# Layer normalisation of five row tiles moved to GpSimd, statistics in one stretch, scheduler numbers refitted

## Chip, cores and metric

One core of one Trainium2 chip. The metric is the device time of one execution in microseconds, the slowest core (here the only one). The kernel before took 181.99 us (median of 3 runs, 181.78 to 183.0).

## The reference, cut to what matters

```python
def _layernorm(x, axis=-1, eps=1e-5):
    m = jnp.mean(x, axis=axis, keepdims=True)
    v = jnp.var(x, axis=axis, keepdims=True)
    return (x - m) / jnp.sqrt(v + eps)

# A: gated long convolution over S = 2048 for each of D = 640 channels (by Fourier transform)
# B: token-mixing MLP
h = _layernorm(x)                                        # x: (1, 2048, 640)
u = gelu(einsum("bsd,sf->bdf", h, w1) + b1)              # w1: (2048, 1536)
y = einsum("bdf,fs->bds", u, w2) + b2
# result: g * a + (1 - g) * y^T,  g = sigmoid(sum(x * gate_w))
```

`x` lies in SBUF as 16 row tiles of 128 x 640 in bf16, called X, four to each block `hk`. The first MLP product adds over the 2048 rows, so a finished sum needs all 16 normalised tiles.

## The kernel before

The whole kernel is one list of operations. Before anything is emitted, a list scheduler *in the kernel file* walks it with assumed durations and writes the order in which each engine will execute. At run time each engine keeps that order and waits on semaphores. So a wrong duration does not change what is computed; it changes the order.

The parts that matter:

```python
free = {e: 2.4 if e == "ACT" else 0.0 for e in engs}     # when each engine begins, in the model
dma_free = 0.0
...
def ts(eng, o, a, s1, s2, op0, op1=None, mode=1, prio=None, extra=0.0):
    n = n_of(o)
    d = dve_dur(n, mode) + extra if eng == "DVE" else n / 900.0 + 0.2    # assumed us on GpSimd
    ...
def ln_tile(hk, p):      # two bn_stats of 320 columns and one bn_aggr, VectorE
    ...
def ln_scale(a, b):      # GpSimd: var + eps, power -0.5, and their product
    ...
def ln_apply(a, b):      # VectorE: X = (X - mean) * rstd, one tile each
    ...
# for h in (0, 1): transp(h, db) ...; after the first half's transposes
#   consts()             # PE turns the bias rows b1, b2, which come by small DMAs
#   fwd(...)             # forward Fourier products of the filter ("W")
for t in range(8):
    ln_tile(t // 4, t % 4)
for t in range(8, 12):
    ln_tile(t // 4, t % 4)
lnlast.append(SC.ops[-1])
ln_scale(0, LNA)                       # LNA = 8
ln_apply(0, LNA)
lnlast.append(SC.ops[-1])
for t in range(12, 16):
    for o_ in ln_tile(t // 4, t % 4):
        o_.after.update(lnlast[-1:])
ln_scale(LNA, 16)
ln_apply(LNA, 16)
lnlast.append(SC.ops[-1])
```

## Time and profile before

| | before |
|---|---|
| time, median | 181.99 us |
| span in the profile | 179.7 us |
| PE busy / idle | 173.1 / 6.6 us |
| first unbroken forward product (chain of waits) | 13.18 us |
| PE's last matmul ends | 177.06 us |
| X tiles 0 to 3 normalised | about 21.4 us |
| X tiles 8 to 15 normalised | 30.1 to 33.0 us |

PE and DVE (VectorE) are both near 95% busy. ACT is ScalarE, POOL is GpSimd. "GT" is the gelu's output, "ksh" the shifted keys, "wT" the turned filter, "rows" the bias rows, "rstd" the inverse deviation.

### The profile page before, as it was taken

The page shows a single profiled execution, that of the slowest core. Times are in us where ns is not written, and L with a number is a line of the kernel's source. Part 1 is how long each engine was busy: PE and PEld are TensorE (multiplying, and loading weights), DVE is VectorE, ACT ScalarE, POOL GpSimd, SP SyncE. Part 2 cuts the span into 40 slices and gives each one's busy share as a digit, 9 for nine tenths or more (in the row PEclk, how much of TensorE's full clock was granted, in tenths as well). Part 3 has the DMA queues.
Part 4 walks back from the last instruction along what each step waited for, and adds up shares of the span by engine and source line. Part 5 has one row for each costly group of instructions (what it writes and reads, how often), then busy time and mean ns, then how long its engine had stood idle before and what let it go on. Part 6 is the DMA issues. An engine that isn't in the chain of part 4 may idle for free.

```text
span 179.7 us, 3335 instructions
## 1 busy us (share of the span) xinstructions
PE 173.1 (96%) x1381; PEld 128.7 (72%) x1381; DVE 171.2 (95%) x203; ACT 116.9 (65%) x176; POOL 43.7 (24%) x42
## 2 busy tenths in 40 slices
PE   7969998899999999999999999999999999999993
PEld 2546785587778777776777778888888887777772
DVE  7999895999999999999999899999999999999984
ACT  5899998899898999617999932131231323753760
POOL 4089404190000054000240010402525000252000
PEclk9999999999999999999999999999999999999999
DMA  6999999999999999998299969797999999599463
GB/s 151 381 411 372 388 294 194 268 420 296 212 258 286 184 271 248 229 228 218 60 243 299 197 94 365 170 225 253 166 193 217 210 200 385 218 154 240 116 233 135
DMA packets 38542, 43.51 MB, mean 242 GB/s; under 512 B 15867, under 2 KB 31360, under 8 KB 38528
## 3 DMA queue, kind: packets, MB, share of 16 engines
q1 hardware_dynamic: 33296, 32.16, 58.2%
q0 software_dynamic: 5200, 11.14, 35.6%
q8 instruction: 11, 0.18, 0.4%
q14 instruction: 3, 0.02, 0.0%
q10 hardware_dynamic: 32, 0.01, 0.0%
HBM read 25.87 MB, written 2.62 MB: 159 GB/s over the span
## 4 chain that ended last, share of the span: by engine, by line
PE 88%; ACT 10%; DVE 0%; issue 0%
PE pp L295 88%; ACT wT L670 3%; ACT C L670 2%; ACT ksh L670 2%; ACT FTB L670 2%; ACT L670 1%; ACT GT L670 0%; DVE O L682 0%; DVE zz L686 0%; ACT cw L670 0%; DVE cst L686 0%
## 5 line engine op out<-in xcount | busy, mean ns | idle before, releaser
L295 PE MATMUL pp<-X,ring 128*128 128x320 bf16 x384 | 55.6, 299 | 0.0
L626 DVE TENSOR_TENSOR C<-C 128x2560 bf16<-128x2560 bf16 (+2 forms) x37 | 54.5, 1521 | 0.0
L295 PE MATMUL pp<-GT,W 128*128 128x320 bf16 x384 | 52.6, 299 | 0.0
L295 PEld LDWEIGHTS pp<-GT,W 128*128 128x128 bf16 x384 | 43.6, 114 | 8.6
L295 PEld LDWEIGHTS pp<-X,ring 128*128 128x128 bf16 x384 | 37.1, 98 | 14.9 <-DVE X L641 0.7
L670 ACT ACTIVATE C<-pp 128x640 bf16<-128x640 f32 x64 | 40.4, 723 | 4.9 <-PE pp L295 4.9
L670 ACT ACTIVATE O<-pp,c,omg 128x640 bf16<-128x640 f32 x15 | 13.3, 884 | 34.7 <-PE pp L295 34.7
L264 POOL DMA_DIRECT2D C<-C x8 | 10.9, 1610 | 41.7 <-DVE C L626 38.3
L295 PE MATMUL pp<-wT,FTB 128*128 128x320 bf16 x112 | 17.2, 299 | 2.5 <-ACT wT L670 1.4
L670 ACT ACTIVATE cgb<-pp,gg 128x640 bf16<-128x640 f32 x16 | 12.7, 794 | 5.7 <-PE pp L295 5.3
L295 PEld LDWEIGHTS pp<-wT,FTB 128*128 128x128 bf16 x112 | 10.5, 98 | 7.7 <-ACT wT L670 1.8
L670 ACT ACTIVATE GT<-pp,cc 128x640 bf16<-128x640 f32 x12 | 9.6, 799 | 9.0 <-PE pp L295 9.0
L626 DVE TENSOR_TENSOR tm<-C,C 128x2560 bf16<-128x2560 bf16 (+1 forms) x7 | 14.3, 2057 | 0.0
L922 DVE BATCH_NORM_STATS2 stats<-X 128x6 f32<-128x320 bf16 x32 | 13.5, 461 | 0.0
L295 PE MATMUL pp<-C,FTB 128*128 128x320 bf16 x96 | 13.4, 299 | 0.0
L264 POOL DMA_DIRECT2D C<-q_hi x6 | 5.9, 977 | 27.7 <-DVE C L626 13.2
L295 PEld LDWEIGHTS pp<-C,FTB 128*128 128x128 bf16 x96 | 9.3, 98 | 3.8 <-issue 0.3
L670 ACT ACTIVATE gq<-gq 128x640 bf16<-128x640 bf16 x16 | 11.8, 741 | 0.0
L626 DVE TENSOR_TENSOR SS<-C 128x2560 bf16<-128x2560 bf16 x8 | 11.7, 1487 | 0.1
L626 DVE TENSOR_TENSOR C<-tm 128x2560 bf16<-128x2560 bf16 (+1 forms) x9 | 10.6, 1192 | 0.1
L670 ACT ACTIVATE ksh<-pp 128x1024 bf16<-128x1024 f32 (+1 forms) x12 | 9.8, 894 | 0.6 <-PE pp L295 0.6
L670 ACT ACTIVATE wT<-pp 128x1024 bf16<-128x1024 f32 x10 | 9.7, 1041 | 0.6 <-PE pp L295 0.6
(73 smaller groups left out, 193.4 us busy)
## 6 DMA issues: line engine op xcount, KB each, us to landing
ring<-in_B_w_dram SPq DMA_DIRECT2D x12, 512.0 KB, 9.6
W<-in_B_w_dram SPq DMA_DIRECT2D x12, 512.0 KB, 6.5
C<-C POOLq DMA_DIRECT2D x8, 640.0 KB, 10.6
X<-in_A_q_dram SPq DMA_DIRECT2D x4, 640.0 KB, 8.4
kn<-in_A_k_dram SPq DMA_DIRECT2D x4, 640.0 KB, 9.3
out_dram<-O SPq DMA_DIRECT2D x7, 320.0 KB, 3.5
C<-SS POOLq DMA_DIRECT2D x3, 640.0 KB, 11.4
ssm<-in_A_ssm_k_dram SPq DMA_DIRECT2D x3, 512.0 KB, 6.8
```

The lines of the kernel that those rows point to most:

```text
L264: ins = engobj.dma_start(out_ap, in_ap, accum_op=ALU.add, max_dma_last_dim=2560)
L295: ins = self.nc.tensor.matmul(ps_ap, lhsT=lhsT, rhs=rhs, start=start, stop=stop, skip_group_check=True)
L626: o_ = SC.add(eng, d, lambda s: T.op(eng, lambda e: e.tensor_tensor(o, a, b, op), rd, [o]), rd, [o], prio=prio, name="tt")
L670: return T.op("ACT", lambda e: e.activation(o, src, func, **kw), rr + [src], ww)
L922: ops.append(SC.add("DVE", 0.38, (lambda o, i: lambda s: T.op("DVE", lambda e: e.bn_stats(o, i), [i], [o]))(o, i), [i], [o]))
```

## The change

Its intent: GpSimd is free from 20 to 28 us. Let it normalise tiles 0 to 4 while VectorE finishes all statistics, so VectorE does not stop between two stretches and has five tiles fewer to normalise. The scheduler's numbers are fitted to the trace at the same time: the engines' beginnings, load rates, the lengths of the transposes, iota and memset costs.

```diff
-        free = {e: 2.4 if e == "ACT" else 0.0 for e in engs}
+        free = {"ACT": 2.93, "DVE": 0.85, "POOL": 0.83, "PE": 1.18, "SP": 0.0, "QA": 0.0}
-        dma_free = 0.0
+        dma_free = 0.3
 ... (ssm_load, x_load: assumed rates)
-  rate=(262.0 if a == 0 else 195.0) if h == 0 else 385.0)
+  rate=({0: 262.0, 1: 223.0}.get(a, RL3)) if h == 0 else 385.0)      # RL3 = 394.0
-  rate=410.0)
+  rate=(352.0 if hk == 0 else 415.0))
 ... (transp: assumed length)
-            m_.dur = 0.5
+            m_.dur = (0.65 + 0.31 * SPIN[db] if h == 0 else 0.55)
 ... (iota, memset: no port lock in the model, iota by its size)
-                for t in range(8):
+                for t in range(16):
                     ln_tile(t // 4, t % 4)
-                for t in range(8, 12):
-                    ln_tile(t // 4, t % 4)
-                lnlast.append(SC.ops[-1])
-                ln_scale(0, LNA)
-                ln_apply(0, LNA)
-                lnlast.append(SC.ops[-1])
-                for t in range(12, 16):
-                    for o_ in ln_tile(t // 4, t % 4):
-                        o_.after.update(lnlast[-1:])
+                    if t == LNA - 1:
+                        ln_scale(0, LNA)
+                lnst = SC.ops[-1]
                 ln_scale(LNA, 16)
-                ln_apply(LNA, 16)
+                for t in PAP:                      # PAP = (0, 1, 2, 3, 4)
+                    xs = X[:, t // 4, t % 4, :]
+                    ts("POOL", xs, xs, mv[:, t, 0:1], rstd[:, t:t + 1], ALU.subtract, ALU.mult, prio=0)
+                lnlast.append(lnst)
+                for t in range(16):
+                    if t not in PAP:
+                        ln_apply(t, t + 1)
                 lnlast.append(SC.ops[-1])
```

More of the change, by code (lines that the diff above doesn't have):

```diff
@@ L683, in last_stt, with nolock @@
             return SC.add("DVE", dve_dur(n_of(o), 1), emit, [sc, b], [o], vt=vt, name="fin")
+        def nolock(*a, **k):
+            o_ = SC.add(*a, **k)
+            o_.lock = False
+            return o_
         def memset(eng, ap, val, prio=None):
-            return SC.add(eng, 0.2, lambda s: T.op(eng, lambda e: e.memset(ap, val), [], [ap]), [], [ap], prio=prio)
+            return nolock(eng, 0.2, lambda s: T.op(eng, lambda e: e.memset(ap, val), [], [ap]), [], [ap], prio=prio)
         def mms(vt, items, prio=None, name="mm"):
@@ L729, in ssm_load @@
         def ssm_load(h, a, b):
-            dma(ssm[:, a:b, 1024 * h:1024 * h + 1024], dr(A_ssm_k, 128 * S * a + 1024 * h, [[S, 128], [128 * S, b - a], [1, 1024]]), 128 * (b - a) * 2048, chain=True, rate=(262.0 if a == 0 else 195.0) if h == 0 else 385.0)
+            dma(ssm[:, a:b, 1024 * h:1024 * h + 1024], dr(A_ssm_k, 128 * S * a + 1024 * h, [[S, 128], [128 * S, b - a], [1, 1024]]), 128 * (b - a) * 2048, chain=True, rate=({0: 262.0, 1: 223.0}.get(a, RL3)) if h == 0 else 385.0)
+        RL3 = 394.0
         def row8(t, hk):
@@ L738, in x_load @@
         def x_load(hk):
-            dma(X[:, hk, :, :], dr(A_q, 512 * hk * D, [[4 * D, 128], [1, 4 * D]]), 128 * 5120, chain=True, rate=410.0)
+            dma(X[:, hk, :, :], dr(A_q, 512 * hk * D, [[4 * D, 128], [1, 4 * D]]), 128 * 5120, chain=True, rate=(352.0 if hk == 0 else 415.0))
         def w1_load(c, hk):
@@ L792, in _build @@
         memset("DVE", cst[:, 1:2], -0.5)
-        iota = lambda ap, pat, b, cm: SC.add("POOL", 0.2, lambda s: T.op("POOL", lambda e: e.iota(ap, pat, base=b, channel_multiplier=cm), [], [ap]), [], [ap])
+        iota = lambda ap, pat, b, cm: nolock("POOL", 0.1 + n_of(ap) / 1100.0, lambda s: T.op("POOL", lambda e: e.iota(ap, pat, base=b, channel_multiplier=cm), [], [ap]), [], [ap])
         iota(dif[:, :], [[1, 128]], 0, -1)
@@ L942, in _build @@
         LNA = 8
+        PAP = tuple(range(5))
         lnlast = []
```

## The prediction

> **What bounds the kernel now.** I read the page first: TensorE (PE) is busy for 96% of the span and VectorE (DVE) for 95%, so neither figure alone says which of them sets the end. The chain of the work that ended last, in order of time, decides:
>
> ```profile
> 13.18 16.41 PE pp L295 x142
> ...
> 30.36 2.02 PE pp L295 x12
> ...
> 32.41 1.30 ACT C L670 x2
> ...
> 33.72 1.28 ACT L670
> ...
> 35.02 0.79 ACT GT L670
> 35.81 1.78 ACT C L670 x3
> 37.59 3.29 ACT ksh L670 x4
> ...
> 40.93 136.12 PE pp L295 x1048
> ...
> 177.08 0.55 DVE O L682
> ```
>
> Columns are start, length and what ran. From 40.93 us to 177.05 the chain is one piece of matmuls, ended by half a microsecond of VectorE. To see whether that piece has slack I cut the span into stages and asked for busy time by stage:
>
> ```profile
> 0.00:13.18 13.18, 10.53 (x74) 5.28 (x74) 12.19 (x34) 10.40 (x11) 5.53 (x12) 1.00 0.86 312
> 13.18:20.80 7.62, 7.62 (x59) 5.39 (x60) 7.02 (x25) 7.01 (x13) 6.85 (x6) 1.00 1.07 378
> 20.80:29.00 8.20, 8.20 (x83) 6.63 (x82) 7.14 (x20) 7.48 (x10) 0.85 (x2) 1.00 1.06 300
> 29.00:41.00 12.00, 10.68 (x124) 7.48 (x122) 10.92 (x15) 10.51 (x15) 6.21 (x3) 1.00 0.99 311
> 41.00:177.06 136.06, 136.04 (x1048) 103.93 (x1048) 133.37 (x111) 81.55 (x129) 24.29 (x21) 1.00 0.94 221
> ```
>
> The columns are the window, its length, then busy time and instructions of PE, PE weight load, DVE, ACT, POOL, then clock, DMA share and GB/s. In the last stage PE runs 1048 matmuls in 136.04 us, at full granted clock. Eighty of them are the short filter matmuls (80 took 4.33 us earlier in the trace, 0.054 us each); the other 968 then take (136.04 - 4.3)/968 = 0.136 us each. Eight X matmuls inside an unbroken stretch take 1.09 us from one block's start to the next block's start, 0.136 us each: the same pace, so this stage is packed. Only what happens before 41 us can move the end. At 0.136 and 0.054 us a matmul the stage 29 to 41 needs 80 x 0.054 + 44 x 0.136 = 10.3 us and takes 12.0: **1.7 us are lost there**. The stage 20.8 to 29 (40 transposes at about 0.054, 43 at 0.136) needs 8.0 of 8.2, and 13.18 to 20.8 is full. The rest of the loss lies before 13.18 us, where the chain runs through ACT (weight transposes and sines), with warm-up matmuls in the gaps.
>
> What the 1.7 us come from is in the timeline of VectorE and GpSimd, by start and length:
>
> ```profile
> 9.79 8.13 POOL L626 TENSOR_TENSOR KF<-cw,m 128x1120 bf16<-128x1120 bf16 x4 [7.00 <-DVE pint L640]
> 17.90 0.25 POOL L640 TENSOR_SCALAR sd<-mv 128x8 f32<-128x8 f32 x1
> 18.23 1.68 POOL L626 TENSOR_TENSOR rstd<-sd,cst 128x8 f32<-128x8 f32 x1
> ...
> 35.27 4.96 POOL L1031 COPY KT<-KT 128x20 bf16<-128x20 bf16 x1 [4.95 <-DMA KT<-kp]
> ```
>
> ```profile
> 19.95 2.94 DVE L641 TENSOR_SCALAR X<-X,mv,rstd 128x640 bf16<-128x640 bf16 x8 [0.57 <-POOL rstd L626]
> ...
> 30.08 2.94 DVE L641 TENSOR_SCALAR X<-X,mv,rstd 128x640 bf16<-128x640 bf16 x8 [2.11 <-POOL rstd L626]
> ```
>
> Row tiles 8 to 15 of X are normalised only from 30.08 to 33.0 us, after a 2.11 us idle wait for the second inverse deviation. The first MLP sums hold two of the four PSUM buffers until all 16 tiles are there. With two buffers left, PE and ACT run by turns: ACT idles 0.88 and 0.86 us for PE, PE idles about as long for ACT.
>
> **What the Trainium skill says.** "SBUF — State Buffer", section "Who interferes with whom": a VectorE instruction with at most one SBUF input outside the two-port modes does not contend with GpSimd; one in a two-port mode, or with two SBUF inputs, does, and the loser blocks fully. The trace agrees on both sides: the four KF multiplies took 2.057 to 2.064 us each, evenly, beside the statistics; the 20-column KT copy took 4.96 us beside back-to-back VectorE tensor-tensors. "GPSIMD Engine Reference", section "3.1 Elementwise — side-by-side cycle accounting", has a light body bound by its port at 1.03 cycles an element; "4.1 Engine selection" calls one-input work roughly line-rate. The trace has no such instruction of this size on GpSimd, but its 896-element memset took 0.83 us, which is near. "Perfetto Trace Analysis", section "Identifying the Most-Contended Engine", warns that matmul busy time is a poor measure of closeness to roofline; hence my counts at a pace instead of 96%.
>
> **The change, part by part.**
> 1. *Statistics in one stretch.* Twelve tiles were done at 19.4 us; a tile costs 0.86 us (two BATCH_NORM_STATS at 0.43 in sequence; tile starts 12.70, 13.56, 14.41). Four more: 19.4 + 3.4 = 22.8, say 23 us, against 27.9 before. Nothing is added; the order changes.
> 2. *Five applies on GpSimd.* Removed from DVE: 5 x 0.36 us (8 took 2.94) = 1.8 us. Added to GpSimd, estimated from the skill's GPSIMD page: 640 x 1.03 / 1.2 GHz = 0.55 us plus some 0.2 us fixed (the 128x8 TENSOR_SCALAR took 0.25), 0.75 us; the kernel's own model says 0.91. I take 0.85 each, 4.3 us. They can begin when the first inverse deviation is ready: GpSimd was on KF until 17.9, then 2.3 us of scale work, so 20.2 us. Tile 3 is then ready at 23.6 and tile 4 at 24.5 or later. DVE delivered tile 3 at 21.4: **the first MLP group comes about 2 us later**.
> 3. *The second half.* GpSimd does the second scale after 23 us: it interleaves with the last apply, 2.3 + 0.9 us after about 23.6, giving the inverse deviation at about 26 to 26.7. DVE spends the wait on tiles 5 to 7 (1.1 us) and two kp copies (1.5 us). Tiles 8 to 15 then take 2.9 us, to about 29.5. **All of X is ready about 3.5 us earlier** than 33.0, and DVE is ahead by about that.
> 4. *Fitted beginnings, loads and iota costs.* They change no instruction and no byte, only the order that the list scheduler writes. I worked through its early ACT order by hand: the second sine should come before the first weight evacuation, but all four sines, five evacuations and the small copy still stand before the first full forward product. The start at 13.18 should stay within 0.3 us.
>
> On the path: of the 1.7 us lost between 29 and 41 I expect 1.2 back, since X no longer holds the sums and ACT gets its work earlier; ACT's own load there (10.51 of 12 us busy) keeps the rest. Between 22 and 24 us PE lacks the X group (1.09 us) that it ran at 21.02. It can pull forward products and transposes ahead, but three conversion buffers and ACT's 0.61 us per evacuation limit that: I charge 0.4 us. Sum: -1.2 + 0.4 = -0.8 us, with the end otherwise unchanged: 181.99 - 0.8 = 181.2 us. DVE's 1.8 us saved and 3.5 us of lead are worth nothing after 41 us, where PE is packed.
>
> **Rivals.**
> - *GpSimd becomes the wait.* For: five applies in a row feed the first MLP groups, two-port DVE applies and kp copies from 23 us contend for the port (KT shows 4.96 us for a small copy), and the second scale queues behind. If an apply costs 1.3 us or the order puts an apply before the power, PE loses 1 to 2 us around 24: about 182.5 us. Against: the statistics do not contend, and DVE must wait for that scale anyway, so it lets go of the port.
> - *All loss recovered, and the opening fitted too.* If sines leave the path before 13.18 (each costs ACT about 1.05 us there) and 1.7 us come back: 179.5 us. Against: the sines' priorities are not in the change, and five evacuations plus four sines fill ACT from 5.15 to 13.13.
> - *DVE is the hidden bound, so its 1.8 us count in full.* It would give about 180 us. For: 133.37 busy of 136.06. Against: PE is never idle in that stage, and the chain ends in PE.
>
> **Range and chances.** The central case is 181.2 us. The ceiling of the gain in the middle is 1.7 us, with up to 1 us from the opening, so 2% (below 178.35 us) needs more than all of that: 0.04. A loss of 2% (above 185.6 us) needs a new stall of over 4 us, for example a port lock that holds GpSimd: 0.04. Within 2%: 0.92. Range 179.7 to 182.9.
>
> **What would show each step.** BATCH_NORM_STATS in one stretch ending at 22.5 to 23.5 us; GpSimd tensor-scalars on X of 0.75 to 1.0 us each; DVE applies 11 instead of 16, the last ending near 29.5; the unbroken PE piece starting some 0.8 us earlier for the same work and still running to the end; PE idle before 41 us below 1.0 us after the forward products begin. I am wrong if GpSimd's applies take above 1.3 us, if PE shows a wait on X by GpSimd of over 1 us, if the first forward product starts more than 0.5 us off 13.18, or if PE gets gaps after 41 us.

## The result, and the profile after

The changed kernel took **189.36 us** (median of 4 runs, 189.25 to 190.88) against 181.96 (4 runs). The ratio is 1.0414, 95% interval 1.0348 to 1.0479: slower by 4%, outside my range. Ratios here are the mean time of one kernel's fast runs over that of the other's of the same rounds, so not quite the ratio of the medians.

Where the time went, by stage. Kernel before, two stages (columns as in the prediction):

```profile
28.00:42.00 14.00, 12.68 (x138) 8.91 (x137) 11.92 (x16) 12.24 (x17) 7.06 (x4) 1.00 1.01 315
42.00:179.70 137.70, 135.04 (x1042) 103.20 (x1039) 132.92 (x111) 80.55 (x128) 24.29 (x21) 1.00 0.93 217
```

The changed kernel:

```profile
13.00:28.00 15.00, 13.05 (x92) 8.69 (x92) 13.17 (x40) 11.56 (x20) 14.84 (x9) 0.89 1.10 343
28.00:42.00 14.00, 11.21 (x82) 8.12 (x82) 6.83 (x12) 8.59 (x11) 7.58 (x7) 0.88 1.06 334
42.00:50.00 8.00, 7.61 (x105) 6.16 (x104) 8.00 (x8) 7.74 (x12) 0.00 (x0) 1.00 0.33 77
50.00:187.40 137.40, 134.46 (x1037) 102.88 (x1034) 130.16 (x108) 79.49 (x126) 24.30 (x21) 1.00 0.91 212
```

Before, 1042 matmuls are left at 42 us and need 137.7 us to the end of the span; after, 1037 are left at 50 us and need 137.4. So the whole loss stands by 50 us, and the long stage behind it is unchanged. Over the span PE is idle 187.4 - 175.9 = 11.5 us instead of 6.6, and busy for 2.8 us more with the same 1381 matmuls: the granted clock was 0.89 and 0.88 in the two stages before 42 us, 1.00 before.

The chain of the work that ended last now runs through GpSimd before it reaches PE:

```profile
20.15 10.53 POOL X L641 x4
...
30.73 7.52 PE pp L295 x56
```

What holds PE there. PE's timeline of the changed kernel, by start and length (the bracket is the idle time before and who ended it):

```profile
14.11 0.38 PE L295 MATMUL pp<-ident,rows 4*128 4x4 bf16 x5 [2.91 <-DMA rows<-in_B_b_dram]
...
15.68 9.74 PE L295 MATMUL pp<-wT,FTB 128*128 128x320 bf16 x64
...
28.24 0.45 PE L295 MATMUL pp<-X,ring 128*128 128x320 bf16 x2 [1.08 <-POOL X L641]
30.73 0.45 PE L295 MATMUL pp<-X,ring 128*128 128x320 bf16 x2 [2.04 <-POOL X L641]
31.01 2.66 PE L295 MATMUL pp<-ident,ssm 128*128 128x128 bf16 x24
```

Two new waits. The bias matmuls now stand *before* the forward product in PE's order, and the small loads of these rows (4 and 3 KB, issued from 4.7 us on, after seven large loads of `ssm` and X) are there only at 14.1 us. Then the first X matmuls wait tile by tile for GpSimd, with 24 ready transposes behind them in the queue. GpSimd and VectorE in the same kernel:

```profile
20.14 13.02 POOL L641 TENSOR_SCALAR X<-X,mv,rstd 128x640 bf16<-128x640 bf16 x5
33.14 0.25 POOL L640 TENSOR_SCALAR sd<-mv 128x8 f32<-128x8 f32 x1
33.47 1.66 POOL L626 TENSOR_TENSOR rstd<-sd,cst 128x8 f32<-128x8 f32 x1
```

```profile
26.37 1.11 DVE L641 TENSOR_SCALAR X<-X,mv,rstd 128x640 bf16<-128x640 bf16 x3
35.17 2.94 DVE L641 TENSOR_SCALAR X<-X,mv,rstd 128x640 bf16<-128x640 bf16 x8 [7.69 <-POOL rstd L626]
```

The view of the tile X gives the durations, minimum/median/maximum in ns:

```profile
L641 POOL TENSOR_SCALAR X<-X,mv,rstd x5: 2497/2498/3061, 20.1 to 30.7; 128x640 bf16<-128x640 bf16 x5
```

**One apply takes 2.5 us, not 0.85.** Five take 13.0 us. Tile 3 is ready at about 30.7 us (21.4 before), the second scale cannot begin before 33.14, and VectorE idles 7.69 us for it; X is whole at 38.1 us instead of 33.0. The length is not a wait for VectorE: the last two applies, from 28.18 us on, took 2.50 us each while VectorE did nothing. The one of 3.06 us is the third, from 25.13 us, beside a kp copy and VectorE's own applies.

### The profile page after: what moved, and what is told of

Its sections match the earlier page's. It is cut to its first block, busy times and chain, and to the rows that moved or that the text cites. A ratio compares the mean times of both kernels' runs of the same rounds, so it can differ in the third digit from the quotient of the medians.

```text
span 187.4 us, 3336 instructions
## 1 busy us (share of the span) xinstructions
PE 175.9 (94%) x1381; PEld 130.9 (70%) x1381; DVE 170.2 (91%) x198; ACT 117.4 (63%) x176; POOL 52.1 (28%) x47
## 4 chain that ended last, share of the span: by engine, by line
PE 76%; POOL 11%; ACT 6%; DVE 5%; issue 1%; POOLq 0%
PE pp L295 76%; POOL X L641 6%; POOL KF L626 4%; ACT C L670 3%; ACT ksh L670 2%; DVE pint L640 2%; DVE pint L626 1%; POOL rstd L626 1%; ACT L670 1%; DVE stats L929 0%; ACT GT L670 0%; ACT gq L670 0%; DVE O L682 0%; DVE ident L640 0%; DVE rows L808 0%
## 5 line engine op out<-in xcount | busy, mean ns | idle before, releaser
L295 PE MATMUL pp<-wT,FTB 128*128 128x320 bf16 x112 | 17.5, 310 | 0.7 <-ACT GT L670 0.5
L295 PEld LDWEIGHTS pp<-wT,FTB 128*128 128x128 bf16 x112 | 11.0, 102 | 6.7 <-ACT GT L670 0.8
L641 POOL TENSOR_SCALAR X<-X,mv,rstd 128x640 bf16<-128x640 bf16 x5 | 13.0, 2613 | 0.0
L641 DVE TENSOR_SCALAR X<-X,mv,rstd 128x640 bf16<-128x640 bf16 x11 | 4.0, 438 | 7.7 <-POOL rstd L626 7.7
```

The costliest lines, as they stand in the source:

```text
L295: ins = self.nc.tensor.matmul(ps_ap, lhsT=lhsT, rhs=rhs, start=start, stop=stop, skip_group_check=True)
L641: return e.tensor_scalar(o, a, s1, s2, op0=op0, op1=op1)
```

## Experiments

My theory after this (A): the arrival of X, set by five GpSimd applies, sets the end, and the early wait for the bias rows hides behind it. The rival (B): the two losses add. (C): the fits are harmless. Every time below stands beside a run of the kernel before on the same chip, whose medians were 181.86 to 182.24 us.

| run | what it is | median us | ratio to before (95%) |
|---|---|---|---|
| e1 | fits alone | 183.25 | 1.0087 (1.0046 to 1.0128) |
| e2 | layer norm part alone | 190.02 | 1.0445 (1.0427 to 1.0463) |
| e3 | changed, all applies on VectorE | 184.81 | 1.0144 (1.0100 to 1.0187) |
| e4 | changed, bias matmuls later | 189.24 | 1.0413 (1.0379 to 1.0446) |
| e5 | e3 and e4 together | 184.22 | 1.0105 (1.0050 to 1.0161) |
| e6 | five forms of the apply (wrong results) | | |
| e7 | before, second scale split | 182.20 | 0.9996 (0.9972 to 1.0019) |
| e8 | changed, true cost in the scheduler | 191.22 | 1.0493 (1.0460 to 1.0526) |
| e9 | e5 with two tiles on GpSimd | 185.95 | 1.0192 (1.0156 to 1.0228) |
| e10 | changed, half of each of the five tiles | 185.17 | 1.0158 (1.0116 to 1.0200) |
| e11 | before, gelu table early | 181.36 | 0.9953 (0.9936 to 0.9971) |
| e12 | e11, fourth sine later | 181.45 | 0.9970 (0.9942 to 0.9998) |
| e13 | e11 and e7 | 182.37 | 1.0028 (1.0016 to 1.0040) |
| e14 | e12 and e7 | 181.47 | 0.9977 (0.9961 to 0.9993) |
| e15 | before, one stretch of statistics, all on VectorE | 182.89 | 1.0061 (1.0048 to 1.0074) |

### Which part does it: e1 to e5 and e15

**e1.** The changed kernel with the layer norm block of the kernel before.

> Only the fitted scheduler numbers of the change; the layer norm stretch is that of the kernel before (two stretches of statistics, all 16 applies on VectorE). Theory A (the GpSimd applies set the end; the early wait of PE for the bias rows is hidden behind them): standing alone, the early wait of 2.9 us plus a lowered clock for about 4 us must show here in full or nearly, since nothing later hides it: 184 to 185.5 us, first forward product at about 15.7 us instead of 13.2. Theory B (both losses add up in the changed kernel): also about 185, because B says 7.4 = 3.3 + 4. Theory C (the fits are harmless): 182.

Measured 183.25 us, less than A and B had said, but not C's nothing. The mechanism is there:

```profile
14.56 0.38 PE L295 MATMUL pp<-ident,rows 4*128 4x4 bf16 x5 [2.72 <-DMA rows<-in_B_b_dram]
...
15.53 1.66 PE L295 MATMUL pp<-wT,FTB 128*128 128x320 bf16 x11
```

The forward product starts 2.35 us later than in the kernel before (15.53 against 13.18), but the last matmul ends only 1.22 us later (178.28 against 177.06): the slack of the stage around 30 to 40 us gives half of it back. And in the profiled run the clock did not fall. In two of the four runs of e1 it did: they had a mean granted clock of 0.991 and 0.989 and took 184.17 and 183.66 us, the other two 0.999 and 1.0 with 182.84 and 182.69. So the fits cost about 0.9 us without half clock and 2.1 us with it, and the median lies between. The stretch from 16 to 17 us, first of the changed kernel, then of e1 (same columns as before; the granted clock is the number after POOL's busy time and count):

```profile
16.00:17.00 1.00, 1.00 (x5) 0.55 (x4) 1.00 (x6) 0.01 (x1) 1.00 (x1) 0.50 1.06 368
```

```profile
16.00:17.00 1.00, 1.00 (x9) 0.72 (x8) 1.00 (x5) 0.72 (x2) 1.00 (x2) 1.00 1.07 362
```

After 2.91 us of idle PE ran at half clock from about 14 to 17.5 us (five matmuls a microsecond instead of nine); after 2.72 us in e1 it did not.

Why the bias matmuls moved is a matter of order, seen in the instruction lists without a run: putting back the old engine beginnings, the old load rates or the old transpose lengths, any one of the three alone, puts them behind one or more of the first forward products again. The scheduler's model has the bias rows there just before the first forward product can start, so it lets them go first.

**e2.** The kernel before, with only the layer norm part of the diff and its `PAP`.

> The kernel before with only the layer norm part: one stretch of statistics and five applies on GpSimd, the scheduler's numbers as before. Theory A: X tile 3 still comes at about 30.7 us and tiles 8 to 15 at 35 to 38, whatever PE does earlier, so the time stays at 188 to 189.5 us, and PE waits 2 to 3 us longer for X than in the changed kernel. Theory B: 185 to 186 us.

Measured 190.02: A's side, 0.5 us above its figure and far from B's. The forward product starts at 13.62, and PE spends the gain waiting:

```profile
26.13 0.45 PE L295 MATMUL pp<-X,ring 128*128 128x320 bf16 x2 [2.65 <-POOL X L641]
28.67 0.72 PE L295 MATMUL pp<-X,ring 128*128 128x320 bf16 x2 [2.10 <-POOL X L641]
31.16 0.71 PE L295 MATMUL pp<-X,ring 128*128 128x320 bf16 x2 [1.77 <-POOL X L641]
```

It waits 6.5 us for GpSimd's X in all, against 3.1 in the changed kernel, and ends no earlier. The steps of 2.5 us are GpSimd's pace.

**e3.**

```diff
-        PAP = tuple(range(5))
+        PAP = ()
```

> The changed kernel with all 16 applies back on VectorE, all statistics still in one stretch. Both theories: no apply of 2.5 us stands before X any more, so X is whole by about 30 us. Theory A: the early loss shows again, about 184.5 us. Theory B: 189.4 minus about 4, 185.4. If the one stretch of statistics itself is the harm: 187 or more.

Measured 184.81: with the applies back on VectorE two thirds of the loss are gone. The time lies between A's figure and B's and does not choose between them; e2 and e4 do. X is whole at 31.8 us (16 applies in 5.91 us from 25.94).

**e4.** The bias matmuls get the last operation of the first forward group as one they may only start after (`consts()` is called later, with an `after` on that operation).

> The changed kernel with the matmuls that turn the bias rows held back until the first forward products have begun, nothing else. The forward product should start at about 13.5 us instead of 15.7 at full clock. Theory A: X by GpSimd still arrives at 30.7 us, so 188.5 to 189.5 us, the 2 to 3 us won are spent waiting for X. Theory B: 186 us.

Measured 189.24, the same as the changed kernel: A. The forward product now starts at 13.48 us, and PE waits 5.6 us for X from GpSimd instead of 3.1. Undoing a true loss gave nothing while a longer one stood beside it.

**e5.** e3 and e4 together.

> The changed kernel with both suspected causes taken out: all applies on VectorE and the bias rows turned after the first forward products. What is left of the change is the one stretch of statistics and the rest of the fits. If the two causes are all: 182 to 183 us (within 0.5% of before). If the one stretch has a cost of its own, because the first X tile comes at 26 us instead of 20: 183.5 to 184.5 us.

Measured 184.22, no clear gain over e3 (the intervals overlap). About 1% stays. In its profiled run the second filter load came late (PE waited 0.8 us for it) and the forward product started at 15.16 us, so this run does not show the early fix at its best.

**e15** asks where that 1% sits: the scheduler numbers of the kernel before, one stretch of statistics, `PAP = ()`.

> The kernel before with its own scheduler numbers and only the one stretch of statistics, all applies on VectorE. It tells what the 1% is that stayed when both large causes were undone. If the stretch itself costs, because the first X tile comes at 26 us instead of 20 and PE has nothing in between: 183.5 to 184.3. If the fits cost it, through the order they write: 181.5 to 182.3.

Measured 182.89, ratio 1.0061, outside both figures: a cost of its own, smaller than I said. X is whole earlier (30.3 us), but the first X matmuls come at 26.0 us instead of 21.0, and all forward products and transposes stand before them. So the parts are, in ratios: fits alone +0.9%, one stretch alone +0.6%, both +1.4% (e3); GpSimd applies on top of the stretch +3.8% (e2 less e15), on top of stretch and fits +2.7% (the change less e3), since there they hide the early wait.

### What makes an apply slow, and does the cost scale: e6, e10, e9, e8

**e6.** The five tiles in five forms. Its output is wrong, which doesn't matter for the time.

```diff
+  tile 0: ts(xs, xs, mean, rstd, subtract, mult)     # as in the change
+  tile 1: ts(xs, xs, mean, None, subtract)
+  tile 2: ts(xs, xs, 0.01, 20.0, subtract, mult)     # constants
+  tile 3: tt(xs, xs, xs, mult)
+  tile 4: 320 columns as tile 0; 320 columns ts(20.0, None, mult)
```

> Wrong results on purpose. In the changed kernel the five tiles on GpSimd get five forms: two operations with two per-row scalars on 640 columns; one operation with one per-row scalar; two operations with constants; a tensor-tensor multiply of the tile with itself; then 320 columns with two per-row scalars and 320 columns with one constant operation. If the cost is per element of the two-operation body, halves take half, and one operation clearly less than 2.5 us, say 1.3. If it is reading the scalars from memory, the constant form falls to about 0.9 us. If it is bf16 conversion and the software loop, all forms stay at 1.8 to 2.5 us for 640 columns. Tensor-tensor: 640 x 1.84 ns = 1.2 us by the four KF multiplies.

GpSimd's timeline in e6 (tiles 1, 2, 3 and one half of 4, which did not need the scale, came first):

```profile
11.90 1.89 POOL L640 TENSOR_SCALAR X<-X,mv 128x640 bf16<-128x640 bf16 x1
13.87 2.36 POOL L641 TENSOR_SCALAR X<-X 128x640 bf16<-128x640 bf16 x1
16.31 1.25 POOL L626 TENSOR_TENSOR X<-X 128x640 bf16<-128x640 bf16 x1
17.64 1.02 POOL L640 TENSOR_SCALAR X<-X 128x320 bf16<-128x320 bf16 x1
```

And its groups by shape from 28 to 31 us:

```profile
L641 POOL TENSOR_SCALAR X<-X,mv,rstd 128x640 bf16<-128x640 bf16 x1 | 2.9, 2873 | 0.0
L641 POOL TENSOR_SCALAR X<-X,mv,rstd 128x320 bf16<-128x320 bf16 x1 | 1.4, 1437 | 0.0
```

Reading scalars from memory is not it: constants take 2.36. A single operation takes 1.89, two 2.36 to 2.5 (2.87 for the first of them here, which overlapped VectorE's applies). So most of the cost is the tensor-scalar form itself, per element: from 320 to 640 columns (1.43 in e6, 2.50 in the changed kernel) it is 1.06/320 = 3.3 ns an element and about 0.4 us fixed. A *two-input* tensor-tensor on the same tile, in bf16 too, takes only 1.25 us, so bf16 alone is not the reason. Of my guesses in the expectation the last, "all forms stay at 1.8 to 2.5", fits every tensor-scalar of 640 columns; why this form is slower than a tensor-tensor no run shows.

**e10.** GpSimd takes columns 0 to 319 of the five tiles, VectorE the rest; the scheduler's order apart from that follows the same wrong rate.

> The changed kernel with GpSimd normalising only columns 0 to 319 of the five tiles and VectorE the other halves; the scheduler still counts GpSimd at its wrong rate. An apply should take about 1.3 us instead of 2.5, tile 3 come at 25.4 to 26 us and all five be done by 27. Arrival theory: the GpSimd part of the loss (189.4 against 184.8 with all on VectorE) nearly vanishes: 184.5 to 185.8. If the loss goes by the number of GpSimd instructions: 189.

Measured 185.17, as A said: 4.2 us less than the changed kernel. The five halves took 8.28 us in all, from 20.56 to 28.8, 1.43 us each at the fastest and more beside VectorE's copies, so longer than the 1.3 I expected. The loss goes with the time that GpSimd takes, not with the number of its instructions. One reserve: PE's order changed too. Its first X matmuls now stand behind all 40 transposes and start at 29.48 us.

**e9.** e5 with `PAP = (6, 7)` and `n / 260.0 + 0.2` for the assumed GpSimd cost.

> The kernel of both undone causes, but with two tiles, 6 and 7, given to GpSimd and their cost counted as 2.66 us in the scheduler. They are needed late, so the wait of X that five tiles caused should be gone; but two applies keep GpSimd until about 25.5 us, just before the second scale can begin. Arrival theory: within 1 us of the kernel with none on GpSimd (184.2), so 183.2 to 185.2. If any GpSimd apply harms, through the port it shares with VectorE, in proportion to its number: 186 us.

Measured 185.95: my arrival figure missed (183.2 to 185.2), the other figure is met. But the run does not decide it. The new cost also changed PE's order: forward products of the second half went before the first X matmuls, and PE waited 2.9 us for ScalarE's weight evacuations there (of 4.4 us in all; the other 1.5 us, before the first product, are in e5 too), at half clock afterwards, from about 29.5 to 32.5 us. X was ready before PE asked for it. I count this run as undecided on what two applies cost.

**e8.** The changed kernel with only the assumed GpSimd cost set right (`n / 260.0 + 0.2`, 2.66 us).

> The changed kernel with one number in its scheduler model changed: a GpSimd tensor-scalar of 640 columns is counted as 2.66 us instead of 0.91. Five applies stay on GpSimd. If the wrong number alone did the harm, through a PE order that waits for X: well under 186 us. If the arrival of X itself is the harm, the order can only fill the wait with forward products of the second half: 186 to 188.5 us.

Measured 191.22, slower than the changed kernel and outside both figures. The order no longer waits for X on PE; instead it runs second-half products, for which ScalarE's evacuations are late (2.8 us of waits), and the first X matmuls start at 34.66 us. Still PE is done earlier: its last matmul ends at 183.4 us, in the changed kernel at 184.7. What makes the run slower is the other end of the kernel. There the new order puts the last inverse Fourier products, whose result ScalarE and VectorE must still gate, at the very end of PE's work:

```profile
178.88 4.51 PE L295 MATMUL pp<-SS,FTB 128*128 128x320 bf16 x32
```

The changed kernel has 32 matmuls behind them, which hide the gating. From PE's last matmul to the end of the span e8 takes 5.7 us, the changed kernel 2.7. With the old end e8 would have taken about 188.1 us (189.4 less 1.3, an estimate that no run tests), inside the arrival figure. So the true number in the model helped PE a little but did not save a plan whose data come late, and it spoiled the order of a distant stage.

### Was there 1.7 us to be had: e7, e11 to e14

**e7.** On the kernel before: tiles 8 to 11 get their scale on GpSimd right after the first.

```diff
-                ln_scale(0, LNA)
-                ln_apply(0, LNA)
+                ln_scale(0, LNA)
+                ln_scale(LNA, 12)
+                ln_apply(0, 12)
 ...
-                ln_scale(LNA, 16)
-                ln_apply(LNA, 16)
+                ln_scale(12, 16)
+                ln_apply(12, 16)
```

> A try for a better kernel, on the kernel before: the second scale is split, so tiles 8 to 11, whose statistics are ready at 19.4 us, are scaled on the idle GpSimd at 20.2 us and applied right after tiles 0 to 7; only tiles 12 to 15 wait for the last scale. Theory: 32 X matmuls more can be had before 30 us, PE loses 0.7 to 1.2 us less between 29 and 41 us: 180.8 to 181.3 us. Rival: ACT holds that stretch, so nothing: 181.7 to 182.

Measured 182.20: the time is near the rival's, but ScalarE is not shown to be the reason. PE's last matmul ends at 176.2 us, 0.8 us before that of the kernel before (177.0), which is what the theory asked of PE. The end of the kernel takes it back as in e8: only 12 matmuls stand behind the last inverse Fourier products instead of 24. Kernel before, then e7:

```profile
173.62 3.42 PE L295 MATMUL pp<-GT,W 128*128 128x320 bf16 x24
```

```profile
174.42 1.79 PE L295 MATMUL pp<-GT,W 128*128 128x320 bf16 x12
```

The chain of e7 leaves PE at 174.6 us and ends in the gating, and from PE's last matmul to the end of the span it takes 4.0 us instead of 2.7. No run has the split with the old end.

**e11.** On the kernel before, a one-column gelu after the last weight evacuation of the second half:

```diff
+    pre_ = act(gth[:, 0:1], cst[:, 0:1], ACT.Gelu_apprx_tanh, prio=0)   # after the sines and that evacuation
+    pre_.dur = 1.4
```

> A try for a better kernel, on the kernel before. Its loss between 29 and 41 us is a stretch in which ScalarE is full and holds a 1.28 us table load before the first gelu. Here a one-column gelu right after the last weight evacuation brings the table in at about 28.7 us, where ScalarE idled 0.88 us. Theory (ScalarE holds the stretch): 0.4 to 1.0 us won, 181.0 to 181.6. Rival (X tiles 8 to 15 hold it): the same as before.

Measured 181.36, ratio 0.9953: a small, clear gain. ScalarE's timeline in e11:

```profile
29.01 1.28 ACT L670 ACT_TABLE_LOAD   x1
30.30 0.20 ACT L670 ACTIVATE gth<-cst 128x1 f32<-128x1 f32 x1
...
33.75 0.80 ACT L670 ACTIVATE GT<-pp,cc 128x640 bf16<-128x640 f32 x1
```

The first real gelu runs at 33.75 instead of 35.02 us. Now PE waits 0.56 us for X tile 8, at 30.66.

**e12.** e11 with the fourth sine held behind the start of the last weight evacuation of the first half (`sins[3].after`).

> The same, and the fourth sine held back until the last weight evacuation of the first half has begun. That sine stands on ScalarE's path to the first forward product: it should start at about 12.2 us instead of 13.2. If PE then stays fed: another 0.5 to 1.0 us, 180.2 to 181.0. If the late sine only moves the loss behind 13 us, where ScalarE evacuates: nothing more than the early gelu.

Measured 181.45, no better than e11. The forward product starts at 12.28 instead of 13.44 us, and PE then waits 1.13 us for X at 30.68: the same end.

**e13, e14.** e11 and e12, each with the split of e7.

> The kernel before with the early gelu table and the split second scale together. Taken alone the split won nothing and the early table 0.5%, after which PE waited for X tile 8 until 30.66 us. Theory (two bounds side by side between 29 and 41 us, ScalarE with its table load and X): together they win more than their sum, 0.8 to 1.3 us, 180.8 to 181.2. Rival (the split costs what it wins): as with the early table alone, 181.4.

> The same with the fourth sine after the last weight evacuation, which brought the first forward product from 13.4 to 12.3 us but then ran into the wait for X (1.13 us at 29.55 to 30.68). Theory: with X tiles 8 to 11 there early, that lead now reaches the end: 179.8 to 180.6 us. Rival (ScalarE's evacuations take it back): 180.9 to 181.3.

Measured 182.37 and 181.47: both theories missed, and the split costs beside the early table (e13 is slower than e11 by 0.75%). The cost again lies in the end that the split writes: PE's last matmul comes at 176.4 us in e13 and 175.1 in e14, against 176.6 in e11 and 177.0 before, but 12 matmuls stand behind the last inverse Fourier products and the rest takes 4.1 and 4.0 us instead of 2.7. With the old end e14 would take about 180 us (181.9 less 2.0, an estimate that no run tests), its theory's figure. In e14 the forward product starts at 12.15 us, tiles 8 to 11 are early, and PE is ahead; then, late in the kernel, this (e13 has the same wait):

```profile
149.91 6.27 PE L295 MATMUL pp<-C,FTB 128*128 128x320 bf16 x45 [0.81 <-DVE C L626]
```

PE waits for VectorE, which its chain shows at work nearly without a break from 113 to 150 us. So one more bound lies close behind: VectorE's own long stretch begins only when X is whole, at 32.4 us in e14 against 32.9 before. e11 remains the best version, 0.5% below the kernel before and within 2% of it; that is 4.2% below the changed one by the medians (181.36 against 189.36).

## Why the prediction was wrong, step by step

- **What bounds the kernel.** Right: the stage behind the early one is packed, and it takes as long after the change as before.
- **Step 2, five applies on GpSimd.** This is the step that failed. The mechanism, "the first MLP group comes later", was named; its size was off. The term was 0.75 to 0.91 us an apply, taken as 0.85; it measured 2.50 (the third one 3.06). Tile 3 came at 30.7 instead of 23.6 us, and 0.4 us charged to PE became 3.1 us of waits for X and more behind them. My bridge was a memset and a 128x8 instruction of the trace and a rate in the skill; none of them is a tensor-scalar over 640 columns.
- **Step 1, the statistics.** They ended at 26.5 us, not 23. I put the two kp copies after them; in VectorE's order they stood inside, one waited 1.28 us for its load, and each took 1.24 us beside GpSimd's applies instead of 0.81. This was not on the path, since GpSimd was busy to 33.1 us. As a part by itself the one stretch cost 0.6% (e15), which I had not charged at all.
- **Step 3, the second half of X.** Whole at 38.1 us, not 29.5: GpSimd did all five applies before the second scale, 13.0 us instead of 4.3.
- **Step 4, the fits.** "The start at 13.18 should stay within 0.3 us" was wrong: it came at 15.68. I followed ScalarE's order by hand and not PE's, where the bias matmuls moved. By itself this costs 0.9% (e1); in the changed kernel it costs nothing measurable, for it hides behind X (e4).
- **The sum.** Of the 1.7 us between 29 and 41 us I called 1.2 recoverable by an earlier X alone. In the changed kernel X came later, so nothing could come back. Where X did come earlier, in e7, PE's last matmul moved forward by 0.8 us, but the time did not change, for the order at the end of the kernel took it back; the early table won 0.9 us by the medians (e11), both together less (e13). "With the end otherwise unchanged" held for the changed kernel (2.7 us after PE's last matmul, as before), not for every order.
- **The rivals.** "GpSimd becomes the wait" was right in kind. It allowed 1.3 us an apply and 182.5 us; the true figure is twice that. The rival in which VectorE's saved time counts in full fell: VectorE is busy 1.0 us less and the kernel is slower. The rival with a better opening fell too: the opening came 2.5 us later.
- **What would show me wrong** named applies above 1.3 us, a PE wait on GpSimd's X above 1 us and a moved forward product: all three happened. The fourth sign, gaps after 41 us, shows only because the early stage itself reaches to 43 us (waits of 0.51 and 0.24 us for ScalarE). The chance of 0.04 for slower was the real error of judgement, with an unmeasured duration in five places on the path.

## What to carry to other kernels

Before work is moved to an idle engine, measure that very instruction there, in shape and form, and multiply it through to the first consumer; an idle engine is only free if its result is not what the busiest engine asks for next. When an order is written from assumed durations, a corrected number can move something far away to the head of a queue, so compare the orders of all engines to the very end, not only the one and the stage in mind: e7 won 0.8 us on PE and lost it in its last four microseconds. If undoing a visible wait changes nothing, look for the longer one that ran beside it, and expect another behind that.

## What the Trainium skill lacked or had wrong

- "GPSIMD Engine Reference", sections "3.1 Elementwise — side-by-side cycle accounting" and "4.1 Engine selection": one-input work is called roughly line-rate and a light body bound at 1.03 cycles an element. A tensor-scalar on 128x640 bf16 took 1.89 us with one operation and 2.36 to 2.50 with two; at the page's 1.2 GHz the slope of 3.3 ns is 4.0 cycles an element. The page has no figure for this form. A two-input tensor-tensor of the same shape took 1.25 us, 2.3 cycles an element, near the page's 2.6 (for f32), so here the one-input form was the slower one.
- "SBUF — State Buffer", section "Who interferes with whom": the direction agrees. Beside GpSimd's applies a VectorE copy took 1.24 us instead of 0.81; the GpSimd power took 2.36 us instead of 1.68 beside VectorE's applies (e3). The extent does not: the page has one of the two fully blocked for the whole instruction of the other, but in the changed kernel that copy ran from 22.95 to 24.19 us, inside a GpSimd apply from 22.64 to 25.14, and three VectorE applies ran at their usual 0.37 us inside the next one, which took 0.56 us longer. In which mode VectorE ran them the trace does not say. What the page lacks is how long back-to-back VectorE work can hold off a tiny GpSimd instruction: the 20-column copy of KT took 0.27 us in e9 with VectorE idle, 4.96 in the kernel before and 12.05 in e11, over several VectorE instructions each. In e13 it took 4.26 us and ended at 37.77, just after VectorE's row of tensor-tensors paused at 37.64. That VectorE's work is what holds it off is inferred; no run isolates it.
- "TensorE: Matmul & The Clock Gate", section "What's actually happening": the page gives a free-running window of 3413 ns and half clock after at least one idle window. Here less idling was enough: half clock followed gaps of 2.91 us (changed kernel) and 1.83 us (e8), both shorter than that window, and none followed 2.72 us (e1). So no fixed length of a gap decides; what does, the runs do not show. Half clock lasted about 3.4 us in the changed kernel and in e8, about one window, and about 6.8 us in e2, where PE went on waiting.
